# Attention, then a max-out FFN: batch 0 scored by halves of the queries, the first twelve FFN units in two token parts

## The chip, the cores and the metric

The kernel runs on one core of a Trainium2 chip. The metric is device time in microseconds for one execution; lower is better. The engines are TensorE (PE, with its weight loads PEld), VectorE (DVE), ScalarE (ACT), GpSimd (POOL) and SyncE (SP, which here only issues DMAs). They run side by side, each through its own queue in order, and wait for each other by semaphores.

## What is computed

```python
# q, k, v: [8, 8, 576, 64]   beacon_k, beacon_v: [8, 8, 16, 64]
k_all = concatenate([beacon_k, k], axis=2)        # 592 keys
v_all = concatenate([beacon_v, v], axis=2)
scores = q @ k_all.T / sqrt(64)                   # causal over k; the 16 beacons are always seen
a = softmax(scores)
x = (a @ v_all).transpose(0, 2, 1, 3).reshape(4608, 512)
h = max(x @ w1, x @ w2, x @ w3)                   # [4608, 768]
out = h @ w_out                                   # [4608, 512], fp32
```

## The kernel before

Heads are taken by quads of four, so there are 16 quads Q, two for each of the 8 batches. Operands are cast to bf16. A quad's queries and keys are brought in by rows, cast (`cast_qk`) and turned by DVE's 32x32 transposes (`turn`) into `qT` and `kT`, three buffers of each, used in rotation. The first two quads are loaded as fp32 by SP and cast on an engine; all others are cast by the DMA itself, issued on POOL (`load_qk16`).

**Scores.** Keys stand in five tiles of 128 (t = 0 to 4), queries along the columns; tile t needs only queries from `q_min[t]` on (0, 112, 240, 368, 496). `bursts` is the list of score steps: a step fills up to 512 columns for each of four heads. `emit_scores` makes the matmuls of a step, eight for each piece (four heads, two halves of the head dimension, 32 rows each, the four heads side by side in the array). In the first steps the heads are taken two by two, so that the first half of a step can be used early. `emit_exp(0)` and `emit_exp(1)` then take the exponential of two heads each on ACT into `at_sb`, and `emit_masks` zeroes the causal edge on POOL. Two PSUM tiles hold one step's scores, so the next step's matmuls wait for the exponentials.

**PV.** For the first two batches (`N_APART` quads) each quad is done in six passes (`pv_pass`): two halves of the queries (288 each), and for each half the sums (part 0, by a matrix of ones) and two interleaved halves of the head dimension. Part 0 ends in a logarithm and an exponential on ACT, which make the reciprocal; the others end in a multiplication on DVE into `xT`, the transposed input of the FFN. Later quads use `pv_segment`, which does all three parts in one set of banks.

**FFN.** `units` is the list of FFN work over 9 blocks of 512 tokens: 18 first-layer units (`mm1_unit`, four 512-column matmuls, evicted by a copy for w1 and by `tensor_max` on DVE for w2 and w3) and four second-layer units (`mm2_unit`, six matmuls, a copy, and a DMA out). For block 0 the 18 are sorted by weight, so that the first six need only w1. `last_unit` is the last second-layer unit, in two halves.

**Order.** Nothing is scheduled by a planner: the text of `emit_all` is the order of each engine's queue. It walks the score steps k; at each it emits scores, exponentials, masks, waiting PV work, what `plan` and `heads` hold for that step (loads, casts, turns), and as many FFN units as `allowed` permits, which grows by 2 a step from step 8 on, and after batch 1 by 2.6 and then 3.4. The first FFN unit comes after the first steps of batch 1. Ahead of all, `spare(17)` puts 17 matmuls on zeros (512 columns each) into PE's queue, with no one reading their result.

Of the kernel before, what the change touches and what calls it, by code (L numbers as in the profile page):

```python
# [16 lines left out]
def kernel(  # L17
# [53 lines left out]
    for Q in range(NQ):  # L71
        apart = Q < N_APART
        pos = 0
        if Q <= N_APART:
            room = 0
        for group in by_burst[0 if apart else 1]:
            if apart:
                room = 0
            for t, q0, q1 in group:
                at_piece.setdefault((Q, t), []).append((q0, q1, pos))  # L80
# [7 lines left out]
    AT_W = pos  # L88
# [14 lines left out]
    vst_pool = ctx.enter_context(tc.tile_pool(name="vst", bufs=2))  # L103
# [3 lines left out]
    nrm_pool = ctx.enter_context(tc.tile_pool(name="nrm", bufs=2))  # L107
    ffn_h = ctx.enter_context(tc.tile_pool(name="ffn_h", bufs=2))
# [29 lines left out]
    for x in first32:  # L138
        nc.gpsimd.memset(x, 0.0)
# [49 lines left out]
    def cast_qk(Q, which, cast, s0=0, s1=QS):  # L189
# [4 lines left out]
        if s1 == QS:  # L194
            stage.pop((Q, which))

    def turn(Q, which, s0=0, s1=QS):
# [6 lines left out]
        if s1 == QS:  # L204
            stage.pop((Q, which, 16))
# [3 lines left out]
    def load_v(b, queue=None):  # L209
        queue = queue or nc.sync  # L210
# [3 lines left out]
        for t in range(n_kt):  # L214
# [43 lines left out]
    def emit_scores(k):  # L258
# [6 lines left out]
        for heads in ((0, 1), (2, 3)) if burst[0][0] < n_quad else (range(HG),):  # L265
# [50 lines left out]
    def pv_pass(Q, hf, part):  # L316
        b, g = divmod(Q, n_quad)
        at_sb, v_sb = at[Q], v_tiles[b]
        h0, h1 = hf * HALF, (hf + 1) * HALF
# [6 lines left out]
        ps = pv_pool[0].tile([128, HALF], FP32, name="pv")  # L326
# [15 lines left out]
        if part == 0:  # L342
            lnd = nrm_pool.tile([128, S - SPLIT], FP32, name="lnd")[:, 0:HALF]
            nc.scalar.activation(out=lnd, in_=ps, func=AF.Ln)
            recip = nrm_pool.tile([128, S - SPLIT], FP32, name="recip")[:, 0:HALF]
            nc.scalar.activation(out=recip, in_=lnd, func=AF.Exp, scale=-1.0)
            recips[Q, hf] = recip
        else:
            c0 = b % RING * S + h0
            nc.vector.tensor_mul(xT[:, 2 * g + part - 1, c0 : c0 + HALF], ps, recips[Q, hf])  # L350
# [61 lines left out]
    def pv_pairs(Q):  # L412
        if Q >= N_APART:
            return [[(Q, 0)], [(Q, 1)]]
# [312 lines left out]
```

## Time and profile before

| | us |
|---|---|
| median of three runs | 287.48 (287.34 to 288.59) |
| the profiled execution | 286.83 |
| its span, first to last instruction | 284.9 |
| PE busy | 273.2 |
| DVE, ACT, POOL busy | 171.4, 157.2, 88.4 |
| mean granted TensorE clock | 0.976 |

The profile shows one execution. Busy time of PE is the time in which a matmul is under way, and since matmuls are pipelined it is not PE at its peak. In a timeline each row has its start in us from the span's start, the time until the end of its last instruction, the engine, the line, the operation with the tiles it writes and reads, the shape of its first instruction, how many are merged in it, and in brackets the idle time of the engine ahead of it with what ended it. A row of matmuls can hold pieces of several widths; the shape is that of the first. In a windows view the columns after the stretch are its length, PE's busy time and instructions, the granted clock as a share of full speed, the DMA engines' share, and GB/s.

### The profile page before, as it was taken

The page shows a single profiled execution, that of the slowest core. Times are in us where ns is not written, and L with a number is a line of the kernel's source. Part 1 is how long each engine was busy: PE and PEld are TensorE (multiplying, and loading weights), DVE is VectorE, ACT ScalarE, POOL GpSimd, SP SyncE. Part 2 cuts the span into 40 slices and gives each one's busy share as a digit, 9 for nine tenths or more (in the row PEclk, how much of TensorE's full clock was granted, in tenths as well). Part 3 has the DMA queues.
Part 4 walks back from the last instruction along what each step waited for, and adds up shares of the span by engine and source line. Part 5 has one row for each costly group of instructions (what it writes and reads, how often), then busy time and mean ns, then how long its engine had stood idle before and what let it go on. Part 6 is the DMA issues. An engine that isn't in the chain of part 4 may idle for free.

```text
span 284.9 us, 7997 instructions
## 1 busy us (share of the span) xinstructions
PE 273.2 (96%) x3393; PEld 134.5 (47%) x3431; DVE 171.4 (60%) x298; ACT 157.2 (55%) x246; POOL 88.4 (31%) x165
## 2 busy tenths in 40 slices
PE   7699999999999999999999999999999999999995
PEld 3246444534545454445454545445454644444442
DVE  4727769856675766656656575666544465554553
ACT  5796576457784766556673686376647630210210
POOL 0483862235553523153415340442134100000000
PEclk9856999999999999999999999999999999999999
DMA  7999999689944954159056913380031003003004
GB/s 247 234 187 203 138 181 206 98 156 251 222 74 122 221 105 84 41 171 197 2 85 196 208 14 73 148 174 3 0 113 39 2 2 134 13 2 147 1 0 147
DMA packets 51923, 33.06 MB, mean 116 GB/s; under 512 B 41264, under 2 KB 42288, under 8 KB 51888
## 3 DMA queue, kind: packets, MB, share of 16 engines
q1 hardware_dynamic: 41152, 20.40, 27.6%
q0 software_dynamic: 10464, 12.01, 26.3%
q8 instruction: 26, 0.43, 0.6%
q10 hardware_dynamic: 272, 0.15, 0.2%
q14 instruction: 9, 0.07, 0.1%
HBM read 35.13 MB, written 9.44 MB: 156 GB/s over the span
## 4 chain that ended last, share of the span: by engine, by line
PE 91%; ACT 3%; issue 1%; DMA 1%; DVE 1%; ACTq 0%; DVEq 0%
PE fps L438 36%; PE sc L273 12%; PE fps L458 11%; PE pv L387 10%; PE pv L438 7%; PE sc L438 6%; PE pv L334 4%; ACT at_sb L288 3%; PE pv L458 2%; PE sc L458 2%; DMA first<-in_beacon_k_dram 1%; PE sc L387 1%; DVE xT L350 0%; ACTq L158 0%; DVE hT L451 0%
## 5 line engine op out<-in xcount | busy, mean ns | idle before, releaser
L288 ACT ACTIVATE at_sb<-sc 128x1024 bf16<-128x1024 f32 (+7 forms) x128 | 103.7, 861 | 31.8 <-PE sc L273 31.6
L438 PE MATMUL fps<-xT,w_sb 128*128 128x512 bf16 x447 | 113.3, 380 | 2.5 <-issue 1.6
L438 PEld LDWEIGHTS <-w_sb 128*128 128x128 bf16 x648 | 59.8, 98 | 74.5 <-issue 6.9
L304 POOL TENSOR_SCALAR_AFFINE_SELECT at_sb<-at_sb 128x512 bf16<-128x512 bf16 (+6 forms) x89 | 47.5, 551 | 127.4 <-ACT at_sb L288 119.0
L451 DVE TENSOR_TENSOR hT<-hT,fps 128x512 bf16<-128x512 bf16 x79 | 54.0, 685 | 33.9 <-PE fps L438 28.1
L273 PE MATMUL sc<-qT,kT 32*128 32x288 bf16 (+15 forms) x960 | 39.7, 266 | 2.9 <-ACT at_sb L288 2.5
L446 ACT CAST hT<-fps 128x512 bf16<-128x512 f32 x34 | 19.9, 586 | 29.9 <-PE fps L438 22.7
L458 PE MATMUL fps<-w_out_sb,hT 128*128 128x512 bf16 x144 | 34.7, 380 | 0.4 <-issue 0.3
L403 DVE TENSOR_TENSOR xT<-pv,recip 128x240 bf16<-128x240 f32 (+1 forms) x46 | 18.8, 450 | 25.5 <-ACT recip L398 24.9
L458 PEld LDWEIGHTS <-hT 128*128 128x128 bf16 x210 | 19.8, 98 | 25.6 <-DVE hT L451 1.7
L273 PEld LDWEIGHTS <-kT 32*128 32x128 bf16 x960 | 19.4, 94 | 22.3 <-issue 16.4
L396 ACT ACTIVATE lnd<-pv 128x240 f32<-128x240 f32 (+1 forms) x23 | 9.4, 408 | 29.8 <-PE pv L387 29.8
L466 DVE COPY y<-fps 128x512 f32<-128x512 f32 x25 | 17.3, 691 | 12.6 <-PE fps L458 12.2
L200 DVE STREAM_TRANSPOSE kT<-c 128x256 uint32<-128x256 uint32 (+1 forms) x32 | 22.0, 707 | 3.2 <-ACT c L193 3.1
L438 PE MATMUL pv<-xT,w_sb 128*128 128x512 bf16 x87 | 22.5, 379 | 0.2
L438 PE MATMUL sc<-xT,w_sb 128*128 128x512 bf16 x83 | 21.5, 380 | 0.1
L200 DVE STREAM_TRANSPOSE qT<-c 128x256 uint32<-128x256 uint32 (+1 forms) x32 | 21.5, 701 | 0.0
L387 PE MATMUL pv<-at_sb,v_sb 128*32 128x160 bf16 (+7 forms) x808 | 20.2, 243 | 0.0
L387 PEld LDWEIGHTS <-v_sb 128*32 128x32 bf16 (+1 forms) x864 | 16.3, 97 | 1.3
L226 POOL CAST v_sb<-vst 128x1024 bf16<-128x1024 f32 (+1 forms) x18 | 15.7, 894 | 0.5 <-issue 0.5
L451 DVE TENSOR_TENSOR hT<-hT,pv 128x512 bf16<-128x512 bf16 x15 | 10.3, 688 | 7.5 <-PE pv L438 4.1
L451 DVE TENSOR_TENSOR hT<-hT,sc 128x512 bf16<-128x512 bf16 x14 | 9.6, 687 | 7.6 <-PE sc L438 6.9
(54 smaller groups left out, 152.9 us busy)
## 6 DMA issues: line engine op xcount, KB each, us to landing
out_dram<-y SPq DMA_DIRECT2D x35, 256.0 KB, 2.0
vst<-in_v_dram SPq DMA_DIRECT2D x21, 256.0 KB, 4.8
c<-in_k_dram POOLq DMA_DIRECT2D x14, 288.0 KB, 4.9
c<-in_q_dram POOLq DMA_DIRECT2D x14, 288.0 KB, 6.0
w_sb<-in_moe_w_dram POOLq DMA_DIRECT2D x3, 768.0 KB, 8.6
vst<-in_v_dram SPq DMA_DIRECT2D x7, 224.0 KB, 3.5
vst<-in_v_dram SPq DMA_DIRECT2D x7, 160.0 KB, 6.9
w_out_sb<-in_moe_w_out_dram POOLq DMA_DIRECT2D x1, 768.0 KB, 10.1
```

The costliest lines, as they stand in the source:

```text
L200: nc.vector.transpose(dst.rearrange("p (t s) -> p s t", s=RUN)[:, s0:s1], src.rearrange("p (s d) -> p s d", d=DP),)
L226: cast(v_tiles[b][0:n, t0:t1].rearrange("p t h d -> p (t h d)"), stage["v", b][0:n, t0:t1].rearrange("p t h d -> p (t h d)"),)
L273: nc.tensor.matmul(sc[h // 2][:, h % 2, off : off + w], kT[hs, 128 * t : 128 * (t + 1), j], qT[hs, q0:q1, j], start=(j == 0), stop=(j == 1 ...
L288: nc.scalar.activation(out=at[Q][:, 2 * i : 2 * i + 2, a0 : a0 + w], in_=sc[i][:, :, off : off + w], func=AF.Exp, scale=scale,)
L304: nc.gpsimd.affine_select(out=view, in_=view, compare_op=ALU.is_ge, fill=0.0, base=q0 - (128 * t - Nb), pattern=[[0, HG], [1, edge - q0]], ...
L387: nc.tensor.matmul(pv_banks[32 * j : 32 * j + 32, c : c + w], lhsT, at_sb[0:r, j, a : a + w], start=(t == 0), stop=all(x[1] // BANK != c / ...
L403: nc.vector.tensor_mul(xT[:, 2 * g + part - 1, c0 : c0 + n], pv_banks[:, offs[part] : offs[part] + n], recip,)
L438: nc.tensor.matmul(ps[:, o0 : o0 + n], w_in[i][:, ct, 128 * ft : 128 * (ft + 1)], xT[:, ct, x0 : x0 + n], start=(ct == 0), stop=(ct == n_c ...
L446: nc.scalar.copy(hT[:, ft, :], ps)
L451: nc.vector.tensor_max(hT[:, ft, :], hT[:, ft, :], ps)
L458: nc.tensor.matmul(ps, hT[:, ft, 128 * tt : 128 * (tt + 1)], w_out_sb[:, ft, :], start=(ft == 0), stop=(ft == n_ft - 1),)
L466: nc.vector.tensor_copy(y, ps)
```

## The change

Five things change.

1. Batch 0's scores come by halves of the queries: for each of its two quads (`main`) a step with queries 0 to 287 of key tiles 0 to 2, one with queries 288 to 511 of tiles 0 and 1, and one with 288 to 511 of tiles 2 to 4. The last 64 queries of both quads (`rest`) come after, packed in full steps together with batch 1, whose quads are now done as all later ones (`whole`, `pv_segment`). There are 14 steps before batch 2 instead of 16. The PV passes of batch 0 cover queries 0 to 287 and 288 to 511, and a new `pv_rest` does the last 64 queries of both quads at once.
2. The first twelve FFN units (block 0, w1 and w2) are done in two parts, tokens 0 to 287 and 288 to 511 (`emit_part`, "u" in the order); some use the PV banks as accumulators.
3. Everything up to the end of batch 1 is written out by hand in `emit_first`, one letter for each kind of work. Zeros ("x") of 256 columns instead of 512 stand between the first scores, passes and casts: 37 ahead of the first score and 18 in eight places after it. Casts are spread anew (the first key half on POOL, the second on DVE, the second quad's keys on ACT), w1 and w2 are loaded ahead of the third quad's keys and queries, and one reciprocal is taken on DVE.
4. The first memsets move from POOL to DVE, the staging buffers for values go from two to one, reciprocals get four buffers of their own, and after batch 1 the rate of FFN units is 2.6 and then 3.2.
5. `last_unit` copies its first half on DVE and the two quarters of its second half on ACT and DVE, each with its own DMA.

In the order, "S k" is the scores and the first exponentials of step k, "E k" its second exponentials and masks, "s Q h" a sums pass, "p Q h part" a PV pass, "r" `pv_rest`, "g" and "h" a `pv_segment` and its end, "C" a cast, "t" a turn, "k", "v", "w", "n" loads, "c" a cast of values, "b" and "B" beacon keys, "f" a whole FFN unit. The names and arguments are those of the code.

```diff
-    by_burst = [
-        [[(0, 0, HALF), (3, q_min[3], S)], [(1, q_min[1], S)], [(2, q_min[2], S)]]
-        + [[(0, HALF, S), (4, q_min[4], S)]],
-        [[(t, q_min[t], S) for t in range(n_kt)]],
-    ]
+    main = [[(t, q_min[t], HALF) for t in range(3)]]
+    main.append([(0, HALF, TOKB), (1, HALF, TOKB)])
+    main.append([(2, HALF, TOKB), (3, q_min[3], TOKB), (4, q_min[4], TOKB)])
+    rest = [[(t, TOKB, S) for t in range(n_kt)]]
+    whole = [[(t, q_min[t], S) for t in range(n_kt)]]
...
+    order = [(Q, main) for Q in range(n_quad)] + [(Q, rest) for Q in range(n_quad)]
+    order += [(Q, whole) for Q in range(n_quad, NQ)]
...
-        for heads in ((0, 1), (2, 3)) if burst[0][0] < n_quad else (range(HG),):
+        for heads in ((0, 1), (2, 3)) if k < n_quad * len(main) else (range(HG),):
...
+    def pv_rest(part):
+        n_r = S - TOKB
+        if part == 0:
+            bank = pv_pool[0].tile([128, 512], FP32, name="pv")[:, 0 : 3 * n_quad * n_r]
+            rest_tiles.append(bank.rearrange("p (g c n) -> p g c n", g=n_quad, c=3))
+        ps = rest_tiles[0]
+        for Q in range(n_quad):
+            for t in range(n_kt):
...
+                for j in range(HG):
...
+                    nc.tensor.matmul(
+                        ps[32 * j : 32 * j + 32, Q, part],
+                        lhsT,
+                        at[Q][0:n, j, a : a + n_r],
...
+    N_PARTS = 12
+    def emit_part(part, by_dve, in_pv):
+        tb, ft, i = units[parts_done[part]][2]
+        parts_done[part] += 1
...
+        t0, t1 = ((0, HALF), (HALF, TOKB))[part]
+        pool, name = (pv_pool[0], "pv") if in_pv else (ffn_psum, "fps")
+        ps = pool.tile([128, TOKB], FP32, name=name)[:, 0 : t1 - t0]
+        for ct in range(n_ct):
+            nc.tensor.matmul(
+                ps,
+                w_in[i][:, ct, 128 * ft : 128 * (ft + 1)],
+                xT[:, ct, t0:t1],
...
     def spare(n):
-
         ps = ffn_psum.tile([128, TOKB], FP32, name="fps")
         for _ in range(n):
-            nc.tensor.matmul(ps, zeros[:, 0:128], zeros, start=True, stop=True)
+            nc.tensor.matmul(ps[:, 0:256], zeros[:, 0:128], zeros[:, 0:256], start=True, stop=True)
 
     def begin():
-        spare(17)
...
+        orders = (
+            "C 0 1 1 1; C 0 1 0 2; t 0 1 0; x 4; t 0 1 1; C 0 0 0 0; C 0 0 1 0; x 30; B 0; t 0 0 "
+            "0; t 0 0 1; C 1 1 2 0; x 3; C 1 0 2 2; S 0; t 1 1 0; t 1 1 1; B 1; x 2; E 0; x 5; t "
+            "1 0 0; S 1; E 1; w 0; k 3 0; t 1 0 1; x 4; w 1; c 0 3; S 3; E 3; x 1; s 0 0; p 0 0 "
+            "2; c 3 4; S 5; E 5; x 2; x 1; p 0 0 1; s 1 0 1; S 2; E 2; x 2; k 2 1; p 1 0 2; k 2 "
+            "0; S 4; x 1; E 4; p 1 0 1; s 0 1; b 2; c 4 5; u 0; s 1 1; u 0 1; p 1 1 2; p 0 1 1; S "
+            "6; E 6; k 3 1; p 0 1 2; p 1 1 1; u 0 1; u 1 2; u 1 1; v 1 0 1; t 2 1 0; t 2 1 1; w "
+            "2; u 0; u 1 2; u 1 2; b 3; u 0; t 2 0 0; u 0 2; t 2 0 1; u 1; u 0; u 0 2; u 1; u 1 "
+            "2; v 1 1 2; S 7; u 0 1 2; u 1 1; E 7; u 1 1 2; u 0; u 1 1; w 3; u 0 1 2; t 3 1 1; S "
+            "8; r 0; t 3 0 0; E 8; u 1 1; v 1 2 3; v 1 3 4; u 0 1; r 1; u 1 1; t 3 1 0; v 1 4 5; "
+            "f; t 3 0 1; k 4 1; S 9; E 9; k 5 1; r 2; f; g 2 0; h 2 0; S 10; k 4 0; E 10; f; n; f "
+            "2; S 11; E 11; k 5 0; f 1; b 4; f; S 12; E 12; t 4 1 1; g 2 1; h 2 1; f 1; S 13; E "
+            "13; t 4 0 0; t 4 0 1; g 3 0; h 3 0; f; f; t 4 1 0; g 3 1; h 3 1 "
+        )
...
+        emit_first()
+        ready = 1
+        allowed = 22.0
+        first_rate, rate = 2.6, 3.2
```

More of the change, by code (lines that the diff above doesn't have):

```diff
@@ L87, with parts @@
                     pos, q0, room = pos + w, q0 + w, room - w
-    AT_W = pos
+                ends[Q] = pos
+    AT_W = ends[0]
+    N_FIRST = min(c for c, x in enumerate(bursts) if x[0][0] == N_APART)
+    def parts(Q):
+        return ((0, HALF), (HALF, TOKB)) if Q < n_quad else ((0, HALF), (HALF, S))
     N_STEP = len(bursts)
```

319 lines of the change are left out of this document (182 added, 137 removed).

## The prediction

> **What bounds the kernel now.** I read the page first, then the windows view cut at the changes of the granted clock, then the timelines of the engines up to 64 us.
>
> ```profile
> span 284.9 us, 7997 instructions
> PE 273.2 (96%) x3393; PEld 134.5 (47%) x3431; DVE 171.4 (60%) x298; ACT 157.2 (55%) x246; POOL 88.4 (31%) x165
> ```
> ```profile
> core 0: us, PE busy (x), PEclk, DMA share, GB/s
> 9.39:12.80 3.41, 2.25 (x19) 1.00 1.07 180
> 12.80:16.21 3.41, 3.09 (x32) 0.50 0.95 184
> 16.21:19.63 3.42, 3.29 (x42) 0.50 1.10 196
> 23.04:26.45 3.41, 3.27 (x72) 0.50 1.08 201
> 29.49:281.60 252.11, 248.80 (x3072) 1.00 0.50 104
> ```
>
> PE is the bound. In the last window it is busy for 248.8 of 252.11 us, so from 29.49 us on only less work, or work begun earlier, can shorten the kernel. Before that PE waits or runs at half clock (PEclk 0.50 from 12.80 to 26.45). The profiled execution took 286.83 us, which is 1.93 more than its span; the three runs have a median of 287.48, 0.65 above it. I sum against the 286.83 and add 0.65 at the end. A measurement of this kernel tells about 0.5% (1.4 us) from no change.
>
> ```profile
> start us, us, engine line op out<-in xcount [idle before <-releaser]
> 1.47 6.05 PE L545 MATMUL fps<-xT 128*128 128x512 bf16 x17 [1.47 <-DVE xT L539]
> 7.78 0.65 PE L273 MATMUL sc<-qT,kT 32*128 32x288 bf16 x16 [0.26 <-DVE qT L200]
> 9.48 0.58 PE L273 MATMUL sc<-qT,kT 32*128 32x464 bf16 x4 [1.05 <-ACT at_sb L288]
> 28.16 1.18 PE L334 MATMUL pv<-at_sb,v_sb 128*32 128x288 bf16 x40 [0.42 <-DVE xT L350]
> 29.49 1.68 PE L438 MATMUL fps<-xT,w_sb 128*128 128x512 bf16 x7 [0.16 <-issue]
> 31.62 1.90 PE L438 MATMUL fps<-xT,w_sb 128*128 128x512 bf16 x8
> 33.46 0.57 PE L273 MATMUL sc<-qT,kT 32*128 32x336 bf16 x8
> 54.34 0.63 PE L273 MATMUL sc<-qT,kT 32*128 32x512 bf16 x8
> 54.90 2.76 PE L458 MATMUL fps<-w_out_sb,hT 128*128 128x512 bf16 x11
> 61.72 0.67 PE L273 MATMUL sc<-qT,kT 32*128 32x16 bf16 x24
> 62.33 1.90 PE L438 MATMUL fps<-xT,w_sb 128*128 128x512 bf16 x7
> ```
>
> At 29.49 batch 0 has all its scores and all its PV passes, and the first FFN unit starts. That is the point to beat.
>
> **The change, part by part: when PE becomes dense.** The new order scores queries 0 to 287 of both quads first (steps S0 for quad 0, S3 for quad 1), then 288 to 511 (S1, S2 and S5, S4), leaves the last 64 tokens for later (step 6 and the head of step 7), and lets FFN parts of 288 and 224 tokens start as soon as their tokens are normalised. The first point from which PE can always find work is the PV pass "s 0 1" (the sums for queries 288 to 511 of quad 0), followed by the first FFN part. What leads there is ACT's queue:
>
> ```profile
> start us, us, engine line op out<-in xcount [idle before <-releaser]
> 3.57 0.62 ACT L193 CAST c<-st 128x512 bf16<-128x512 f32 x1 [1.48 <-DMA st<-in_k_dram]
> 6.12 0.72 ACT L193 CAST c<-st 128x640 bf16<-128x640 f32 x1 [0.25 <-DMA st<-in_q_dram]
> 25.31 0.41 ACT L344 ACTIVATE lnd<-pv 128x288 f32<-128x288 f32 x1 [1.64 <-PE pv L334]
> 25.75 0.44 ACT L346 ACTIVATE recip<-lnd 128x288 f32<-128x288 f32 x1
> 33.97 1.35 ACT L288 ACTIVATE at_sb<-sc 128x672 bf16<-128x672 f32 x2 [0.46 <-PE sc L273]
> 55.06 1.94 ACT L288 ACTIVATE at_sb<-sc 128x1024 bf16<-128x1024 f32 x2 [3.04 <-PE sc L273]
> 8.43 6.51 ACT L288 ACTIVATE at_sb<-sc 128x992 bf16<-128x992 f32 x8 [1.58 <-PE sc L273]
> 8.58 0.76 DVE L193 CAST c<-st 128x1152 bf16<-128x1152 f32 x1 [0.86 <-DMA st<-in_k_dram]
> 12.42 1.25 DVE L200 STREAM_TRANSPOSE qT<-c 128x256 uint32<-128x256 uint32 x2
> 11.90 1.76 POOL L304 TENSOR_SCALAR_AFFINE_SELECT at_sb<-at_sb 128x448 bf16<-128x448 bf16 x3
> ```
>
> Quad 1's key cast moves from DVE to ACT and stands in ACT's FIFO ahead of the first exponential. The keys land just before 8.58, when DVE takes them today; the two ACT casts (0.62 for 512, 0.72 for 640) give 0.10 per 128 elements, so 1.1 for 1152: ACT is free at 9.7, where it begins exponentials at 8.43 today (0.65 after the first score). DVE's longer chain before the first score (it now casts a key half itself) and POOL's cast of the other half hide behind that. Exponentials: 0.97 for 1024 elements, 0.675 for 672, hence 0.86 for 896 and 0.76 for 768. S0 ends at 9.7 + 1.94 = 11.6 and S1 at 13.3. S3 needs quad 1's queries, turned at 13.67 as today (same POOL cast, same transposes), and 0.65 for scores: 14.3. S3 ends at 16.25, the logarithm and its inverse (0.85) at 17.1, S5 and S2 (four of 0.76) at 20.1. Then "s 0 1" waits for the masks of S2; POOL has done with S5's by then: 0.6 per 512 elements (1.76 for three), about 1.2 for 80, 128 and 16 columns of four heads. **PE is dense from 21.3**, 8.2 us before 29.49.
>
> What PE still owes at 21.3, that it had done at 29.49 (28.16 row: 40 matmuls, two passes of 1152 columns, 1.18, so 0.51 ns a column):
> - six passes over 832 columns: 6 x 0.42 = 2.5;
> - the scores of the last 64 tokens, 640 columns: 512 take 0.56 (54.34 to 54.90), so 0.7; narrow pieces add little, since 24 matmuls of 512 columns, pieces of 16 among them, take 0.61 (61.72 to 62.33) against 0.56 for eight. With 20 narrow groups 0.9;
> - `pv_rest`, three times 640 columns: 0.33, the turn-over between kinds of matmul and narrowness, 0.5 each: 1.5;
> - splitting twelve units into 24 parts adds no columns, only a few more turn-overs. Eight 512-column matmuls between scores take 1.84 (31.62 to 33.46). In the tail six in a row take 1.30:
>
> ```profile
> 276.25 1.46 PE L458 MATMUL fps<-w_out_sb,hT 128*128 128x512 bf16 x6
> 277.55 0.81 PE L458 MATMUL sc<-w_out_sb,hT 128*128 128x512 bf16 x3
> ```
>
> that is 0.217 each, so a turn-over costs 0.11 and four or five more cost 0.5.
>
> Sum 5.4. Gain 8.2 - 5.4 = 2.8.
>
> **Loads.** The weights w0 and w1 are now asked for ahead of quad 2's keys and queries:
>
> ```profile
> L187 POOL DMA_DIRECT2D c<-in_q_dram x1: 548/548/548, 20.4 to 20.4; - x1
> DMA to landing us min/median/max: 10.3/11.0/11.6
> L218 SPq DMA_DIRECT2D vst<-in_v_dram x2: 793/857/921, 11.1 to 12.1; - x2
> DMA to landing us min/median/max: 4.1/4.3/4.4
> ```
> ```profile
> c<-in_q_dram POOLq DMA_DIRECT2D x14, 288.0 KB, 6.0
> w_sb<-in_moe_w_dram POOLq DMA_DIRECT2D x3, 768.0 KB, 8.6
> ```
>
> Batch 0's values end at 16.2 (12.1 + 4.1); four quad tensors and two weights follow by 32.0 (the last pair's slower one, 20.4 + 11.6). A weight is 2.67 times a quad tensor (768 and 288 KB), so 9.33 units in 15.8 us, 1.7 each. In the new order w0 lands at 20.7, w1 at 26.9, quad 2's queries (8.33 units) at 30.3. The first part needs w0 at 21.8, the second weight is needed at about 30: both in time. Step 7, the first with quad 2, needs queries turned (1.25): 31.6. PE reaches it after six passes (2.5), step 6 (0.7), fifteen parts (eight of 288 columns at 0.49, seven of 224 at 0.38, by 0.217 for 512: 6.6) and some five turn-overs, 10.3 us after 21.3, also at 31.6. I charge 0.3 for this and small waits on accumulators. DVE stands behind these transposes too, but the parts it then evicts come only after them. The single staging buffer for values costs nothing: each batch is cast before the next is loaded. Batch 1 arranged in full bursts and the rate 3.2 instead of 3.4 only move FFN units between steps, since PE has work in both.
>
> **Tail.** The last copy handles 128 columns on each of two engines instead of 256 on one:
>
> ```profile
> 281.65 0.42 DVE L486 COPY y<-fps 128x256 f32<-128x256 f32 x1 [0.62 <-PE fps L479]
> ```
>
> Between nothing and half of 0.42; I take 0.15.
>
> **Clock, the open term.** All this holds if the clock stays up. Before, it fell at 12.80 after a window in which PE had waits of about a microsecond (9.48 row) and short score bursts. Its two bursts of eight, priced by a dense burst (0.56 for eight of 512 columns, these are narrower), would fill 1.0 of 3.41 us, 30%. In the 3.4 us before it, zeros up to 7.52 and the scores of 7.78 fill about 63%, and the clock held. In the new order the first window has seven zeros partly in it, S1 and four zeros, about 1.2 us or 36%, the next one 42%. That lies inside the bounds and nearer the lower one; but zeros use the whole array, the two-head score bursts half of it, and by rows used it is 15% before, 29% after. The Trainium skill, "TensorE: Matmul & The Clock Gate", section "Why this matters for your kernels", wants no PE-idle gaps over about 3 us; by that rule the clock would hold and the sum stand, but the rule would not have had it fall here, where the longest wait is 1.05. The trace decides against the rule, so I keep both cases.
>
> **The rivals.**
> - Clock falls at 12.80, returns at 23.04. PE then needs 8.1 us instead of 4.05 from S3 (13.7) to "s 0 1" (S3 0.57, S5 and S2 0.43 each, S4 0.5, five passes of 0.27, seven zeros of 0.11), reaching it at 21.8. By 23.04 it has done 0.6 of the work where the forecast has 1.75: 1.15 late.
> - As today, back at 26.45: 2.3 against 5.15, 2.85 late. The zeros then do not do what they are placed for.
> - **Slower:** the mixed PV, score and FFN work does not lift the clock in 23.04 to 26.45 either; it returns a window later, at 29.87: 4.0 against 8.6, 4.6 late. It decides once the return is later than about 26. For it: the windows at 12.80 and 16.21 were nearly all busy and stayed at 0.50; against: a window of mostly PV lifted it at 26.45.
> - Loads: if quad 2's queries need the 11.6 us that today's second pair needed, 21.9 + 11.6 + 1.25 puts step 7 at 34.8, 2.9 later.
> - Narrow matmuls. If some 200 of 64 columns each cost a fixed time, the row at 61.72 (24 in 0.61, 25 ns each) bounds it at 5.0 for the 2.4 counted, 2.6 lost. The Trainium skill, the same page, section "Wait — 56ns, not 53.3ns?", puts start-to-start at no less than about 25 ns; by it the gain is nearly gone. Against it: the 16-column pieces of that row add only 0.05.
>
> **How the numbers follow.** Forecast: 286.83 - 2.8 + 0.3 - 0.15 = 284.2, plus 0.65 = 284.8, chance 0.46. Clock back at 23.04: 286.0 (0.23), at 26.45: 287.6 (0.13), at 29.87: 289.4 (0.06). Loads: 287.7 (0.04). Narrow matmuls: 287.4 (0.04). More gain than summed, down to 283.3 if the 0.3 is not paid and the late columns cost only their streaming, 4.2 instead of 5.4 (0.04). Range 283.3 to 287.9: above it stand the late clock and what of the loads and the clock at 26.45 falls worse than priced. Faster by over 0.5% is below 286.0: 0.46, 0.04 and half of 0.23, 0.62. Slower is above 288.9: the late clock and a fourth of the case at 287.6, 0.09. The rest, 0.29, is the same.
>
> **What would show it.** PEclk stays 1.00 from 6 us on, with zeros between scores; the first exponential near 9.7; an idle ACT from 13.3 to 14.3; the first FFN part near 22 and PE busy from there; step 7 near 32 without a wait on quad 2's transposes; `pv_rest` runs of 0.5. A half clock between 12.8 and 23 to 30 makes the forecast wrong by the prices above; an FFN start after 24 at full clock would mean that ACT's or POOL's queue, not PE's clock, was misjudged.

## The result: 1.0% slower

| | before | after |
|---|---|---|
| median, us | 287.28 (286.26 to 288.59) | 290.16 (288.60 to 292.20) |
| the profiled execution, us | 286.83 | 288.60 |
| its span | 284.9 | 286.9 |
| end of PE's last matmul | 281.61 | 283.50 |

The ratio of the times is 1.0103, 95% interval 1.0057 to 1.0150. The forecast was 284.8 with a range up to 287.9. It had the sign wrong, and the result lies above the range. A few executions in the experiments below are over 1.5% longer than the fastest of their kernel; the ratios leave them out.

The page of the changed kernel, and its windows cut where the clock changed, at step 7 (33.07), at the first scores of batch 2 (57.88) and at the last long wait (94.21):

```profile
span 286.9 us, 8781 instructions
PE 278.1 (97%) x3789; PEld 145.5 (51%) x3789; DVE 171.7 (60%) x307; ACT 159.5 (56%) x256; POOL 90.9 (32%) x169
```
```profile
core 0: us, PE busy (x) PEld busy (x) DVE busy (x) ACT busy (x) POOL busy (x), PEclk, DMA share, GB/s
7.47:14.29 6.82, 5.17 (x78) 3.69 (x78) 4.79 (x11) 4.94 (x6) 3.50 (x6) 1.00 0.89 224
14.29:21.12 6.83, 6.83 (x132) 4.55 (x120) 4.14 (x5) 5.36 (x8) 4.89 (x8) 0.50 1.04 189
21.12:33.07 11.95, 11.75 (x282) 9.58 (x275) 8.00 (x19) 8.33 (x20) 6.35 (x12) 1.00 1.01 169
33.07:57.88 24.81, 24.55 (x543) 14.46 (x543) 18.18 (x37) 16.15 (x27) 11.89 (x21) 1.00 1.08 158
57.88:94.21 36.33, 34.75 (x512) 16.56 (x505) 22.70 (x40) 25.37 (x39) 14.95 (x28) 1.00 0.73 137
```

In the profiled executions zeros did shorten the half clock: two windows of 3.41 us (14.29 to 21.12) instead of four (12.80 to 26.45). Yet the kernel is slower, so the clock alone cannot be the story. The timeline of ACT and PE, beside the times that the forecast gave:

```profile
start us, us, engine line op out<-in xcount [idle before <-releaser]
9.79 3.56 ACT L296 ACTIVATE at_sb<-sc 128x1024 bf16<-128x1024 f32 x4 [0.26 <-PE sc L281]
14.44 1.94 ACT L296 ACTIVATE at_sb<-sc 128x1024 bf16<-128x1024 f32 x2 [1.08 <-PE sc L281]
17.06 1.49 ACT L296 ACTIVATE at_sb<-sc 128x768 bf16<-128x768 f32 x2
19.84 1.51 ACT L296 ACTIVATE at_sb<-sc 128x768 bf16<-128x768 f32 x2 [1.29 <-PE sc L281]
22.36 0.58 PE L342 MATMUL pv<-at_sb,ones 128*32 128x224 bf16 x20
22.87 0.67 PE L502 MATMUL fps<-xT,w_sb 128*128 128x288 bf16 x4
25.48 0.71 PE L281 MATMUL sc<-qT,kT 32*128 32x64 bf16 x64
30.85 1.03 PE L502 MATMUL fps<-xT,w_sb 128*128 128x224 bf16 x8 [0.20 <-issue]
33.07 0.64 PE L281 MATMUL sc<-qT,kT 32*128 32x64 bf16 x24
57.88 0.63 PE L281 MATMUL sc<-qT,kT 32*128 32x512 bf16 x8
75.42 0.50 PE L436 MATMUL pv<-at_sb,v_sb 128*32 128x240 bf16 x16 [1.02 <-POOL v_sb L234]
94.21 3.52 PE L472 MATMUL fps<-xT,w_sb 128*128 128x512 bf16 x14 [0.50 <-DVE xT L452]
```

ACT keeps to the forecast to the first exponentials of step 5 (9.7, 14.3 and 17.1 foretold; 9.79, 14.44 and 17.06 measured). Then it waits 1.29 us for scores that PE makes at half clock, and "s 0 1" comes at 22.36 instead of 21.3. Step 7 comes at 33.07 instead of 31.6. Batch 2 begins at 57.88. Before, it began at 54.34 with 18 FFN units done. Now 21 are done, and the three more are second-layer units of six matmuls at 0.217, 3.9 us together. So 57.88 is worth 53.98 of before: 0.36 us are left of the gain of 2.5 that was forecast for this point. From here to the end of PE's work the kernel before takes 227.27 us (54.34 to 281.61). With 3.9 us less to do, the changed kernel should take 223.4. It takes 225.62. The two waits at 75.42 and 94.21 are 1.52 of these 2.2.

### The profile page after: what moved, and what is told of

It is laid out like the page before. It is cut to its first block, busy times and chain, and to the rows that moved or that the text cites. A ratio compares the mean times of both kernels' runs of the same rounds, so it can differ in the third digit from the quotient of the medians.

```text
span 286.9 us, 8781 instructions
## 1 busy us (share of the span) xinstructions
PE 278.1 (97%) x3789; PEld 145.5 (51%) x3789; DVE 171.7 (60%) x307; ACT 159.5 (56%) x256; POOL 90.9 (32%) x169
## 4 chain that ended last, share of the span: by engine, by line
PE 85%; DMA 9%; DVE 2%; ACT 2%; SPq 1%; issue 1%; POOL 0%; POOLq 0%
PE fps L472 30%; PE fps L521 11%; PE pv L436 10%; PE sc L281 10%; PE sc L472 7%; PE pv L472 6%; DMA vst<-in_v_dram 5%; PE fps L502 3%; PE sc L521 2%; PE pv L342 2%; DMA st<-in_q_dram 2%; DMA st<-in_k_dram 1%; PE pv L502 1%; PE pv L521 1%; DVE xT L452 1%; ACT at_sb L296 1%
## 5 line engine op out<-in xcount | busy, mean ns | idle before, releaser
L296 ACT ACTIVATE at_sb<-sc 128x1024 bf16<-128x1024 f32 (+6 forms) x130 | 102.2, 849 | 19.2 <-PE sc L281 19.2
L472 PE MATMUL fps<-xT,w_sb 128*128 128x512 bf16 x412 | 102.4, 380 | 0.5 <-DVE xT L452 0.5
L472 PEld LDWEIGHTS <-w_sb 128*128 128x128 bf16 x600 | 55.6, 98 | 70.7 <-issue 7.7
L312 POOL TENSOR_SCALAR_AFFINE_SELECT at_sb<-at_sb 128x512 bf16<-128x512 bf16 (+10 forms) x94 | 48.6, 537 | 122.4 <-ACT at_sb L296 119.3
L487 DVE TENSOR_TENSOR hT<-hT,fps 128x512 bf16<-128x512 bf16 (+2 forms) x81 | 53.7, 663 | 30.0 <-PE fps L472 25.4
L281 PE MATMUL sc<-qT,kT 32*128 32x192 bf16 (+21 forms) x1104 | 37.4, 249 | 1.7 <-DVE qT L210 1.3
L485 ACT CAST hT<-fps 128x512 bf16<-128x512 f32 (+2 forms) x34 | 18.9, 555 | 35.5 <-PE fps L472 33.6
L521 PE MATMUL fps<-w_out_sb,hT 128*128 128x512 bf16 x162 | 38.3, 380 | 0.0
L436 PE MATMUL pv<-at_sb,v_sb 128*32 128x160 bf16 (+7 forms) x952 | 23.8, 243 | 1.0 <-POOL v_sb L234 1.0
L487 DVE TENSOR_TENSOR hT<-hT,pv 128x512 bf16<-128x512 bf16 (+2 forms) x18 | 11.1, 616 | 6.9 <-ACT hT L485 2.5
```

The lines of the kernel that those rows point to most:

```text
L281: nc.tensor.matmul(sc[h // 2][:, h % 2, off : off + w], kT[hs, 128 * t : 128 * (t + 1), j], qT[hs, q0:q1, j], start=(j == 0), stop=(j == 1 ...
L296: nc.scalar.activation(out=at[Q][:, 2 * i : 2 * i + 2, a0 : a0 + w], in_=sc[i][:, :, off : off + w], func=AF.Exp, scale=scale,)
L312: nc.gpsimd.affine_select(out=view, in_=view, compare_op=ALU.is_ge, fill=0.0, base=q0 - (128 * t - Nb), pattern=[[0, HG], [1, edge - q0]], ...
L436: nc.tensor.matmul(pv_banks[32 * j : 32 * j + 32, c : c + w], lhsT, at_sb[0:r, j, a : a + w], start=(t == 0), stop=all(x[1] // BANK != c / ...
L472: nc.tensor.matmul(ps[:, o0 : o0 + n], w_in[i][:, ct, 128 * ft : 128 * (ft + 1)], xT[:, ct, x0 : x0 + n], start=(ct == 0), stop=(ct == n_c ...
L485: nc.scalar.copy(hT[:, ft, cols], ps)
```

## The experiments

Three theories. **T1**: the half clock from 14.29 on takes the gain. **T2**: loads, and what stands in the queues behind them, take it, as do FFN units that run out later because they were done earlier. **T3** was formed after the first four runs: PE's own instructions come too late. Medians are given with the ratio to the kernel before, which was measured in turn with them on the same chip (medians 287.0 to 287.5).

### The same kernel; without later zeros; with more; with later loads

Unchanged, for the spread:

> The changed kernel unchanged, for its spread and a second trace. Theory T1 (clock: half clock between about 14 and 21 us sets the loss): runs with a longer half-clock stretch are the slow ones; a run at full clock would be at most 286. Theory T2 (loads: values of batch 2 and the third to fifth quads' tensors land late, and PE waits): the time between runs varies with the length of PE's waits on v_sb and on turned keys, whatever the clock; 288.5 to 292 again.

Measured 290.57, ratio 1.0124 (1.0080 to 1.0168): the result repeats. One of the six executions of the first measurement had the full clock throughout and took 289.53, where T1 allows 286 at most.

Without the 18 zeros after the first score:

```diff
-            "... S 0; t 1 1 0; t 1 1 1; B 1; x 2; E 0; x 5; t 1 0 0; S 1; E 1; w 0; ..."
+            "... S 0; t 1 1 0; t 1 1 1; B 1; E 0; t 1 0 0; S 1; E 1; w 0; ..."   # all later x too
```

> The 18 zero matmuls after the first score are left out, the 37 ahead of it stay. T1: if the zeros hold the clock up at all, the half clock begins at or before 12 to 14 us and lasts to 26 or longer: 1 to 3 us slower than the changed kernel. T2: the early part only sets when PE gets dense; without the zeros PE reaches the first FFN part the same or up to 1 us earlier; within 1 us of the changed kernel either way.

Measured 292.45, ratio 1.0186 (1.0156 to 1.0216): 1.9 us slower than the unchanged kernel, as T1 expected, with the half clock from 12.08 to 25.73 in the profiled execution. That execution also holds a wait of 2.20 us at full clock, shown below.

With 44 of them (5, 11, 9, 3, 5, 3, 5, 3 in the eight places for 2, 5, 4, 1, 2, 1, 2, 1):

> Each group of zeros after the first score is doubled and gets one more (18 become 44). T1: clock at 1.00 throughout, first FFN part 1 us earlier than in the profiled run of the changed kernel (22.9), 1 us faster. T2: no gain from the clock that the end shows, because the later waits on loads stay: within 0.7 us.

Measured 292.87, ratio 1.0175 (1.0137 to 1.0213): a miss for both theories. T1 by itself falls: in the profiled execution the clock stayed at 1.00 from 4.5 to 31.8, and the kernel became slower than with a half clock. Its two executions without any half clock took 290.70 and 290.85.

Quad 7's loads three steps later, so that they do not share a step with quad 6's:

```diff
-            at_step(max(first_step[Q] - 9, N_FIRST), ...)
+            at_step(max(first_step[Q] - (6 if Q == 7 else 9), N_FIRST), ...)
```

> One edit: the loads of quad 7's keys and queries are asked for three score steps later, so that they no longer stand ahead of batch 2's values in the DMA rings (step 14 asks for quads 6 and 7 in one go). T2: the values land 2 to 4 us earlier, the 1.0 us wait of PE on v_sb near 75 us goes: 1 to 3 us faster. T1: no change (within 0.7 us).

Measured 288.96, ratio 1.0063 (1.0036 to 1.0089), 1.6 us below the unchanged kernel measured beside it. This part of T2 holds. In the changed kernel POOL waits for batch 2's values, and PE's wait at 75.42 (above) is for that cast. With quad 7 later, PE has no wait there (first row: POOL in the changed kernel; the others: PE with quad 7 later).

```profile
74.33 1.04 POOL L234 CAST v_sb<-vst 128x1024 bf16<-128x1024 f32 x1 [3.37 <-DMA vst<-in_v_dram]
75.23 0.34 PE L436 MATMUL pv<-at_sb,ones 128*32 128x240 bf16 x8
75.40 0.49 PE L436 MATMUL pv<-at_sb,v_sb 128*32 128x240 bf16 x16
```

In the profiled execution with quad 7 later the clock was full throughout. The next rows, PE and DVE of the kernel with quad 7 later, show that PE then waits for loads and for what stands behind them:

```profile
22.51 0.66 PE L502 MATMUL fps<-xT,w_sb 128*128 128x288 bf16 x4 [0.65 <-DMA w_sb<-in_moe_w_dram]
26.09 0.57 PE L342 MATMUL pv<-at_sb,v_sb 80*32 80x16 bf16 x24 [1.39 <-DVE v_sb L234]
25.07 0.20 DVE L161 CAST bk<-bk 128x64 bf16<-128x64 f32 x1 [3.09 <-DMA bk<-in_beacon_k_dram]
25.62 0.42 DVE L234 CAST v_sb<-vst 80x512 bf16<-80x512 f32 x1
```

The value tile needed at 24.7 had been loaded since 17.1. Its cast ("c 4 5") stood on DVE behind "b 2", which waited 3.09 us for sixteen-row loads of beacon keys that are not used before step 7.

The slower two share something else, waits of PE that no engine ends (timelines of PE without later zeros, and with 44):

```profile
46.84 0.63 PE L281 MATMUL sc<-qT,kT 32*128 32x176 bf16 x22 [2.20 <-issue]
```
```profile
31.63 0.39 PE L502 MATMUL pv<-xT,w_sb 128*128 128x224 bf16 x2 [3.42 <-issue]
31.82 1.91 PE L502 MATMUL fps<-xT,w_sb 128*128 128x224 bf16 x8
33.53 1.70 PE L502 MATMUL pv<-xT,w_sb 128*128 128x224 bf16 x8
```

"issue" says that nothing the profile shows was waited for. The trace has one more kind of record, the packets of the instruction queue (q8 on the page: 29 packets of 16,384 bytes after, 26 before). Set beside the count of PE's matmuls and weight loads (a row is one of either; a few matmul records are missing, so a row is right to within a few), the waits fall into place:

| kernel | PE begins row n - 256 | q8 packet starts | PE begins row n | n | wait |
|---|---|---|---|---|---|
| before | 25.41 | 28.83 | 33.70 | 705 | none |
| after | 25.53 | 28.62 | 30.85 | 961 | 0.20 |
| after, repeated | 21.86 | 24.60 | 27.03 | 705 | 0.39 |
| no later zeros | 39.98 | 44.18 | 46.84 | 1473 | 2.20 |
| 44 later zeros | 25.41 | 29.20 | 31.63 | 961 | 3.42 |

The waits end at rows 705, 961 and 1473, which are multiples of 256 apart, and 2.2 to 2.7 us after a packet of 256 x 64 bytes starts. That packet starts 2.7 to 4.2 us after PE entered the block before. Where PE uses up 256 instructions in less than these two together, it stands. In the order before, rows 449 to 961 last 18.7 us (25.41 to 44.07); in the changed order 10.0 (20.86 to 30.85). This is T3. The DMA engines are as full in the order before (share 1.29 in this stretch, 1.01 from 21.12 to 33.07 after), so they are not what sets the two apart.

### Beacon keys, fewer units, whole units, and zeros in the kernel before

Based on the later quad 7, "b 2" behind the last PV pass of batch 0:

```diff
-            "... p 1 0 1; s 0 1; b 2; c 4 5; u 0; ... p 0 1 2; p 1 1 1; u 0 1; ..."
+            "... p 1 0 1; s 0 1; c 4 5; u 0; ... p 0 1 2; p 1 1 1; b 2; u 0 1; ..."
```

> The changed kernel with quad 7's loads three steps later, and with batch 1's beacon keys ("b 2") behind the last PV pass of batch 0 instead of ahead of the cast of the last value tile ("c 4 5"). In the run with late quad-7 loads DVE waited 3.09 us for these small loads, the cast stood behind it, and PE waited 1.39 us for that cast. Theory T2 (loads and the queues behind them eat the gain): that wait goes, 0.7 to 1.4 us less than with late quad-7 loads alone, ratio 1.001 to 1.004, and step 7 near 32.5. T1 (the early half clock eats it): nothing changes but the clock's luck, ratio 1.006. T3 (PE waits for its own instructions): ratio 1.006, with a wait of PE between 20 and 60 us that no engine ends, in some executions.

Measured 289.10 (286.84 to 295.67), ratio 1.0046 (1.0018 to 1.0074). PE's wait for the cast is gone from the profile, but the time is not told apart from the kernel it is based on: a miss for T2, which expected 0.7 to 1.4 us.

On top of that `first_rate` 2.4 instead of 2.6:

> As the kernel with the beacon keys moved, and with 2.4 FFN units a step instead of 2.6 until batch 2 is done. PE waited 0.50 to 0.72 us near 94 to 99 us for the end of a PV segment in all runs of the changed kernel so far, since the units of finished batches had run out. T2 (units run out): that wait goes and 0.5 to 0.7 us with it, ratio 0.999 to 1.002. If the wait only moves elsewhere: no difference to the kernel with the beacon keys moved.

Measured 292.51, ratio 1.0175 (1.0145 to 1.0205): a miss, and it went the other way. The long wait near 94 is gone; others took its place (PE between 57 and 100, the rows with waits over 0.2):

```profile
69.63 1.02 PE L472 MATMUL fps<-xT,w_sb 128*128 128x512 bf16 x4 [0.74 <-DVE hT L487]
77.95 1.02 PE L472 MATMUL fps<-xT,w_sb 128*128 128x512 bf16 x4 [0.71 <-DVE hT L487]
83.79 0.63 PE L281 MATMUL sc<-qT,kT 32*128 32x320 bf16 x14 [0.35 <-ACT at_sb L296]
```

Before batch 2 is done, PE has a fixed stock of units to put between steps. Spent early, they are missing at 94. Spread thinner, they are missing at 70. This reading is not tested further: the three waits sum to 1.8 us in the fastest of the six executions (290.76), and what the others lose beyond it is in no trace.

The changed kernel with its first twelve units whole (each "u 0" left out, each "u 1" an "f"):

> The changed kernel with the first twelve FFN units whole again (each at the place of its second part). It undoes one part of the change. The prediction held that the 24 parts add no columns and only some 0.5 us of turn-overs, and that they let the FFN start at 21.8. If that start matters: 1 to 2 us slower than the changed kernel, ratio 1.014 to 1.018, with PE waiting 1 us or more around 24 to 27. If the front is set by loads (w0, and quad 2 for step 7): no difference, 1.008 to 1.012. T3 (instructions): 96 instructions of PE fewer before 40 us (48 matmuls and 48 weight loads), so a little less spread.

Measured 290.38, ratio 1.0098 (1.0072 to 1.0124), the same as with the 24 parts: the early parts bring nothing and cost nothing that shows.

The kernel before with zeros between its first scores:

```diff
         for k in range(N_STEP):
             Q = bursts[k][0][0]
+            if 1 <= k <= 7:
+                spare(6, 256)
```

> The kernel before, with six zeros of 256 columns ahead of each of the score steps 1 to 7, nothing else. Zeros between the first scores alone, without the rearrangement. T1 (the clock is what the change can win, and the rearrangement loses it): the clock stays at 1.00 through 12.8 to 26.5, the passes from 19.6 to 26.5 take half the time, the first FFN unit starts near 26 instead of 29.5: 2 to 3.4 us faster, ratio 0.988 to 0.993. T2 (loads): the first FFN unit cannot start before w0 at 24.5, and step 12 not before quad 3 at 32, neither in the way: same as T1. If the zeros stand in PE's way, being ahead of scores, or the clock falls all the same: ratio 1.000 to 1.010.

Measured 287.26, ratio 1.0001 (0.9976 to 1.0025). In the profiled execution the clock was full from 5.5 to the end, and over all twelve nothing was gained: the second blow to T1. Windows and timeline of PE in this kernel:

```profile
19.48:30.24 10.76, 8.24 (x221) 5.77 (x215) 5.91 (x15) 7.92 (x15) 6.36 (x11) 1.00 1.06 193
```
```profile
25.93 0.62 PE L273 MATMUL sc<-qT,kT 32*128 32x288 bf16 x16 [0.48 <-DVE qT L200]
27.54 0.93 PE L334 MATMUL pv<-at_sb,v_sb 128*32 128x288 bf16 x28 [0.42 <-DVE xT L350]
29.64 0.44 PE L334 MATMUL pv<-at_sb,v_sb 128*32 128x288 bf16 x12 [1.18 <-issue]
30.24 1.67 PE L438 MATMUL fps<-xT,w_sb 128*128 128x512 bf16 x7 [0.16 <-issue]
```

At half clock PE was busy 3.27 of 3.41 us there (23.04 to 26.45) and looked like the bound. At full clock it is busy 8.24 of 10.76 and waits for transposes, for DVE, and 1.18 us at row 705, behind a packet that started at 27.22. The first FFN unit comes at 30.24 instead of 29.49, where 0.8 is due to a later start (first scores at 8.57, before at 7.78).

### T3 by dose

Based on the later quad 7 and beacon keys (289.10). Step 6 as one piece, which leaves out the scores of the last 64 tokens of batch 0 and puts others in their place, for time alone; then as sixteen pieces with all scores:

```diff
-            for Q, t, q0, q1, _ in burst:                       # eight pieces of 64 columns
+            for Q, t, q0, q1, _ in [(0, 0, 0, BANK, 0)]:        # step 6, 112 instructions fewer
+            ... for x in range(q0, q1, 32)                      # step 6, 128 instructions more
```

> The kernel with quad 7's loads later and the beacon keys moved, but step 6 is scored as one piece of 512 columns instead of eight pieces of 64: 8 matmuls and 8 weight loads in place of 64 and 64, 112 instructions fewer, with the same 512 columns a head (the scores of the last 64 tokens of batch 0 are left out and others stand in their place, for time alone). T3 (PE's instructions come late between 20 and 34 us, in blocks of 256): the step takes about 0.1 us less, and beyond that PE passes 705 and 961 rows later in its work, so the waits at these rows shrink: step 7 at 32.6 to 33.2 instead of 33.7, 0.5 to 1 us faster than the kernel with eight pieces (289.1), ratio 1.000 to 1.003, and a smaller spread. T2 (loads): 0.1 us at most, ratio 1.004.

Measured 289.18, ratio 1.0039 (1.0007 to 1.0071): no gain, a miss for T3 as it was put. In the profiled execution of the base PE has no wait at rows 705 and 961, so there was none to take away.

> The same kernel as base, but each of the eight pieces of step 6 is cut in two of 32 columns: 64 matmuls and 64 weight loads more, the same columns, the same result. The matmuls themselves take 0.1 to 0.2 us more. T3: half a block of instructions more in the stretch where the supply is just short, so PE waits 1 to 2 us more between 25 and 35, without an engine that ends the wait: 290 to 291, ratio 1.009 to 1.013. T2: 0.2 us more, ratio 1.005.

Measured 294.29, ratio 1.0229 (1.0195 to 1.0264), 5.2 us slower, twice and more what was expected. PE's timeline and windows:

```profile
27.40 1.22 PE L284 MATMUL sc<-qT,kT 32*128 32x32 bf16 x128
31.55 0.73 PE L345 MATMUL pv<-at_sb,v_sb 128*32 128x224 bf16 x32 [2.62 <-issue]
```
```profile
25.67:32.50 6.83, 4.21 (x235) 3.46 (x224) 1.69 (x5) 2.97 (x7) 2.06 (x4) 1.00 0.67 123
32.50:35.91 3.41, 3.41 (x19) 2.50 (x17) 2.43 (x8) 0.66 (x2) 2.08 (x4) 0.50 1.18 133
```

The matmuls of the step took 0.51 us more (1.22 against 0.71). Then PE stood 2.62 us at row 961, 2.50 after the packet at 29.05. And behind that wait the clock was halved for a window, in which PE did 1.7 us of full-clock work in 3.41. These sum to 4.8, of 5.2 between the medians (6.4 between the two profiled executions). So T3 is shown as the main cause of this kernel's loss. The kernel with 44 zeros has the same sequence (half clock from 31.82 to 35.23, behind its wait of 3.42); behind the wait of 2.20 without later zeros the clock stayed full. That the wait brings the half clock is thus seen twice, not tested. For the changed kernel itself the traces show little of T3: its waits at these rows are 0.20 and 0.39.

The base again, with `rate` 3.4 as before:

> The same base with 3.4 FFN units a step after batch 2, as before, instead of 3.2. The prediction counted this part at nothing, since PE has work either way. If so: ratio 1.003 to 1.006, as the base. If units run out ahead of the segments of later batches, waits of 0.5 us or more on xT come back every 33 us or so: 1 to 3 us slower.

Measured 290.05, ratio 1.0084 (1.0054 to 1.0114): some 0.9 slower by the medians, the intervals overlap, between the two things expected. A wait of 0.50 on xT stands at 155.71 that the base does not have.

The kernel before with fewer and wider zeros (`1 <= k <= 5`, `spare(3, 512)`):

> The kernel before with three zeros of 512 columns ahead of score steps 1 to 5 (in the earlier run six of 256 ahead of steps 1 to 7): 15 matmuls instead of 42, 54 instructions fewer, fewer zeros after 17 us. T3: the wait of 1.18 us at row 705 goes or shrinks to under 0.4, the clock stays up, 0.5 to 1 us faster than before, ratio 0.996 to 0.999. T1 (no more than the clock matters): it stays at 1.000, as the clock alone brought nothing. If the clock falls again at 20: 1.000 to 1.003.

Measured 287.06, ratio 0.9973 (0.9947 to 0.9998): as T3 expected, no wait at row 705. The clock did not stay up: it fell for one window in eight of the twelve executions (22.66 to 26.07 in the profiled one) and for two in one.

### Clock and instructions together

Counting half-clock windows in each execution (its lost clock share times its span, by 1.7 us for a window) gives these medians, with the number of executions (the kernel before from all measurements beside the experiments; two long executions of the base, 291.24 and 295.67, are left out):

| kernel | 0 windows | 2 | 3 | 4 | 5 |
|---|---|---|---|---|---|
| before | | 286.41 (2) | 286.82 (43) | 287.62 (31) | 288.39 (22) |
| step 6 as one piece | 286.65 (3) | 289.06 (5) | 290.22 (4) | | |
| base, eight pieces | 289.02 (3) | 288.73 (2) | 288.93 (5) | | |

With fewer instructions, three windows go with 3.6 us more. With all of them the few executions at a full clock show no gain. In the kernel before each further window goes with some 0.8 us. Hence the last test, zeros that cost hardly any instructions (3, 5, 4, 2, 3, 1, 3, 1 of 512 columns for 2, 5, 4, 1, 2, 1, 2, 1 of 256):

> Base is the changed kernel with quad 7's loads later and the beacon keys moved (289.1). After the first score it gets 22 zeros of 512 columns in place of 18 of 256: the same time on zeros as the 44 of 256 tried earlier, with 8 instructions more than the base instead of 52. T1 and T3 together (each half-clock window of 3.4 us costs the new order about 1.2 us, and a late block of instructions takes what a full clock gives): 0 windows in most executions, and no wait of over 1 us near 31: 286.6 to 287.6, ratio 0.997 to 1.001. T3 alone (any faster PE only runs into the supply): waits of 1 to 3 us that no engine ends, 289 to 291. T2 (the remaining loads, w0 at 22 above all): 288.5 to 289, with PE waiting on w0.

Measured 288.46 (287.31 to 289.63), ratio 1.0033 (1.0014 to 1.0052). Every execution had a full clock. It missed the joint expectation by 0.9. The time is that of T2, but its mechanism is not in the profile, where no wait for w0 shows; waits of 0.30 and 0.70 stand at rows 705 and 961. The profiled execution is the fastest of the twelve (287.31).

> The same with step 6 as one piece of 512 columns, 112 instructions fewer (the scores of the last 64 tokens of batch 0 are left out and others stand in their place, for time alone). T1 and T3 together: as the kernel with eight pieces or up to 0.5 us less, 286.3 to 287.0, small spread; what is then left against the forecast of 284.8 is neither the clock nor the instructions. T3 decides beyond that: 1 us or more faster than with eight pieces. T1 alone: no difference to eight pieces.

Measured 287.34 (286.51 to 288.86), ratio 1.0004 (0.9985 to 1.0023), 1.1 below the kernel with eight pieces, as T3 expected, and 1.8 below the one with one piece and fewer zeros. By the medians the two together take away what neither takes away alone (288.46 and 289.18, where the base has 289.10). The two traces do not show where: the profiled execution with one piece took 287.36, that with eight pieces 287.31 with its two waits, and PE's last matmul ends at 282.27 and 282.23.

The best version of the old order, with the new `last_unit`:

> The kernel before with three zeros of 512 columns ahead of score steps 1 to 5, and with the changed kernel's last unit (first half copied on DVE, two quarters of the second on ACT and DVE, each with its DMA). The prediction gave 0.15 us for this last unit, between nothing and 0.2. In the profiles the span ended 3.29 us after PE before and 3.40 after: then it is 0 to 0.1 slower than with the old last unit, ratio 0.996 to 0.999 either way; a version that beats both kernels.

Measured 286.16 (285.75 to 287.29), ratio 0.9960 (0.9942 to 0.9978): 0.4% faster than the kernel before. The last unit is not the reason: in the profiled executions the span ends 3.37 us behind PE's last matmul with it and 3.34 without. The clock is part of it. It was full in eight of the twelve executions here and in three of twelve without the new unit; with a full clock the medians are 286.03 and 286.29, with one half-clock window 287.11 (four) and 287.14 (eight). Why it stayed up more often is not known.

## Why the prediction was wrong

Three steps of the sum failed. "PE is dense from 21.3" came 1.06 us late in the profiled execution; the work owed at that point was 1.07 larger, mainly in the scores (1.64 for the 0.9 of the sum); and what lies behind batch 2's start, put at nothing "since PE has work in both", took 2.25.

What remains when late loads, clock and instructions are taken out is the sum itself. PE's timeline in the last variant of the changed order (22 wide zeros, step 6 as one piece):

```profile
21.90 0.53 PE L342 MATMUL pv<-at_sb,ones 128*32 128x224 bf16 x20
32.49 0.64 PE L281 MATMUL sc<-qT,kT 32*128 32x64 bf16 x24
57.22 0.63 PE L281 MATMUL sc<-qT,kT 32*128 32x512 bf16 x8
77.04 0.74 PE L436 MATMUL pv<-at_sb,ones 128*32 128x336 bf16 x20 [0.57 <-DVE xT L452]
92.99 3.52 PE L472 MATMUL fps<-xT,w_sb 128*128 128x512 bf16 x14 [0.50 <-DVE xT L452]
```

1. **"Before that PE waits or runs at half clock."** This is no term of the sum, but it hid what else bounds the stretch. A PE that is 96% busy at half clock need not be the bound: with narrow zeros the kernel before had the full clock in eight of twelve executions, and over all twelve no time was gained. What stood in the way were DVE's transposes, multiplications on DVE and a late block of instructions. The clock is not worth nothing for that: those eight executions have a median of 287.01, the four with one half-clock window 288.69.
2. **"PE is dense from 21.3."** ACT's chain was right to 0.15 us up to 17.1. The rest was 1.06 late (22.36) with the half clock, and 0.6 late (21.90) in the variant above with a full one, where quad 1's keys had landed late (ACT's cast of them began at 9.14 instead of 8.38).
3. **"Sum 5.4", and 0.3 for waits.** Measured in the changed kernel: 22.36 to 57.88 is 35.52; the kernel before needs 24.85 from 29.49 to 54.34, and three more units are done, 3.9. That leaves 6.8, at full clock without long waits 6.6 (21.90 to 57.22). The term was 0.9 to 1.1 too small. Counted by kind of matmul in the two profiled executions, each from its start to that of the next, the changed stretch is longer by 3.84 for PV, where the sum has 2.5 + 1.5; by 1.64 for scores, where it has 0.9; by 1.1 for first-layer units and waits together, where it has 0.5 + 0.3; and by 4.1 for the three second-layer units. So the scores were mis-sized most. Narrow matmuls were not the reason: step 6's 64 took 0.64 for the 0.56 of a wide burst, so that rival falls in the form it had. The scores of steps 10 to 12 take 0.71, 0.78 and 0.75 instead of 0.57, 0.5 more together:

```profile
42.75 0.78 PE L281 MATMUL sc<-qT,kT 32*128 32x176 bf16 x24
45.45 0.84 PE L281 MATMUL sc<-qT,kT 32*128 32x320 bf16 x16
48.06 0.82 PE L281 MATMUL sc<-qT,kT 32*128 32x272 bf16 x16
```

   In each of them score matmuls start 0.05 or 0.06 us behind the end of an exponential (42.84, 45.62, 48.20), so PE had reached them before ACT freed their buffers. That too few FFN units stand between these steps is the likely reason; it was not tried by itself.
4. **Loads, "I charge 0.3 for this".** w0, w1 and quad 2's queries landed at 21.74, 27.55 and 30.51, near the 20.7, 26.9 and 30.3 of the sum. But the sum looked at batch 0 and 1 only. The collision that cost 1.6 us is at step 14, where quads 6 and 7 are now asked for together, amid batch 2's values (from 61.59 on; the values landed from 73.13 on). I had moved these loads without following the queues behind them.
5. **"Batch 1 arranged in full bursts and the rate 3.2 instead of 3.4 only move FFN units between steps, since PE has work in both."** It has not. This term stood at nothing and took the most, 2.25 behind 57.88: 1.02 the wait for batch 2's values (point 4), 0.50 the end of a segment, when units had run out. The 1.7 us that the last variant loses behind 57.22 (225.05 against 223.4) hold waits of 0.57 and 0.50 for the ends of segments. The rate had no part in these waits, since until batch 2 is done both kernels go by 2.6 units a step; what differs is that 21 units instead of 18 were done before. So work done early was taken from a stock that the stretch up to 94 needed. A lower first rate made it worse, and 3.4 later on was no better.
6. **The clock rivals.** I gave 1.15 for a clock back at 23.04. It was back at 21.12. In executions with step 6 as one piece a window goes with 1.2, three of them with 3.6: three times my price. I had priced only the stretch from 13.7 to 23, which is the likely reason.
7. **Tail, 0.15.** Its mechanism failed: the two quarters do not go side by side. DVE's began when ACT's had ended:

```profile
283.54 0.27 ACT L555 COPY y<-fps 128x128 f32<-128x128 f32 x1 [6.34 <-DMA out_dram<-y]
283.84 0.29 DVE L555 COPY y<-fps 128x128 f32<-128x128 f32 x1 [0.53 <-ACT y L555]
```

   The span ends 3.38 us after PE, 3.31 before.
8. **Not considered at all**: PE's instructions. They are shown to cost time in the kernel with sixteen pieces; in the changed kernel the waits are 0.20 and 0.39. They do not explain the spread: three executions of the base at a full clock lie 3.5 us apart (286.84 to 290.38), those with step 6 as one piece 1.1 (286.64 to 287.70), but with wide zeros and a full clock in all twelve executions the eight pieces spread over 2.3 (287.31 to 289.63) and the one piece as far (286.51 to 288.86).

For the profiled execution the terms are: 1.06 for point 2, 1.07 for point 3, 2.25 behind 57.88 (points 4 and 5), 0.22 for the tail, 4.6 in all; the execution was 4.4 above the 284.2 of the sum (its time is 1.72 more than its span, where the sum has 1.93). It was the fastest of six. The second trace of the changed kernel, at 290.56 near the median, gives the same terms, larger: "s 0 1" at 23.36 is 2.06 late, the stretch to batch 2 at 59.24 is 1.43 longer than summed, and 2.85 are lost behind it, of which 2.36 are its waits for batch 2's values (1.64) and for a segment (0.72). Open is why the clock falls in one window of an execution and not in another, where the remaining 0.6 us behind 57 go (they stand in no long wait), and why the wide zeros with eight pieces still stand 1.1 above those with one by the medians.

## What to carry to other kernels

A full PE at half clock does not yet prove what bounds the stretch: add zeros, few and wide rather than many and narrow, and see whether the end moves. Work pulled forward is a gain only if what it leaves behind is not needed as filler, so follow it to the next place where units run out, and follow every load that is moved to the queue of the next batch. Count PE's instructions as well as its columns where many narrow or short matmuls follow each other: 64 small matmuls more, with their 64 weight loads, cost 5.2 us here.

## What the hardware showed that was not expected

- PE waits for its own instructions, up to 3.42 us, in blocks of 256 matmuls and weight loads, 2.2 to 2.7 us after the start of the block's packet. The profile names it "issue", and where another event ended shortly before, that one: the wait of 0.70 us at row 961 of the kernel with wide zeros is put down to ACT's copy, but ends 2.26 us after a packet like the others. The Trainium skill, "Runtime: NRT & Kernel Launch", section "Instruction fetch mechanics", gives these blocks (16 KiB, 256 instructions, fetched by a DMA queue of the engine's own while the block before runs) and calls the cost of a crossing mostly hidden. The blocks agree with the 256 measured; hidden it is not where PE runs through a block in about 5 us or less. In the wait of 2.62 us the DMA share behind the packet's start was only 0.14, in that of 2.20 it was 1.97, and PE went on 2.50 and 2.66 us after the packet started.
- The clock falls without long waits and comes back in steps of 3.41 us: in the profiled executions of the changed order and its variants where it fell early it did so between 11.68 and 16.48 and was back between 21.12 and 25.73. The Trainium skill, "TensorE: Matmul & The Clock Gate", section "Why this matters for your kernels", asks for no gaps over about 3 us. The half clock behind PE's wait of 3.42 us is in its sense, that behind 2.62 us near it; the one at 14.29, where the longest wait ahead was 0.86 us, is not. In the profiled execution with the first units whole the clock stayed full through waits of 1.31 and 1.22.
- A reciprocal of 288 columns on DVE took 1.96 us, where ACT's logarithm and exponential took 0.42 and 0.44. Here nothing waited for it.
